# Chunk 1's attention scores as three half-precision products, with split K shared over two chunks and a second rectifier on VectorE

## The chip, the core and the metric

The kernel runs on one core of one Trainium2 chip. The metric is the device time of one execution in microseconds (us). The kernel before takes 655.71 us, the median of three runs (654.43 to 657.09). One execution was recorded by the profiler; it took 656.25 us, and its span, from the first to the last instruction, is 654.5 us.

## What is computed

Attention with a learned bias on relative positions, and behind it a layer norm and a two-layer feed-forward net (FFN), all in float32 at the interface. Four batches, eight heads, 576 positions, 64 values per head; the FFN is 512 wide with 2048 hidden values.

```
scores = q @ k.T / sqrt(64)
x      = log1p(|i - j|) / log1p(max(i, 1))            # relative position
bias   = max(x * w1 + b1, 0) @ w2                     # 32 hidden values, one bias per head
attn   = softmax(scores + bias);  a = attn @ v        # per batch and head
y      = (a - mean(a)) / sqrt(var(a) + 1e-6) * g      # over all heads of a position
out    = a + max(y @ w_ch1, 0) @ w_ch2
```

Inputs and outputs are float32, and the products must be nearly as exact. The kernel gets this from float16 in three products: a number is split into a high half-precision part and the residual, and hi*hi + hi*lo + lo*hi is summed in float32. Where it doesn't do so, it multiplies float32 operands, which TensorE executes more slowly.

## The kernel before

**Units.** The 576 query positions are cut into chunks 0 to 3 of 128 rows and chunk 4, the tail, of 64 rows. A visit is one (batch, chunk) pair, and a unit is one head of a visit (in the tail, two heads at once). There are 144 units, numbered in the order of the list `ORD`: the tails of batches 0 and 1, chunk 0, the tails of batches 3 and 2 (units 40 to 47), chunk 1 (units 48 to 79: batches 2, 3, 1, 0), chunk 2 (80 to 111) and chunk 3 (112 to 143). From one chunk to the next the batch stays the same, so its K can be kept.

**One unit.** `qk` multiplies Q and K on TensorE into PSUM; units come in pairs, two at a time. `softmax1` reads the scores and a bias tile on VectorE (line 580, scale and bias added, minimum over the row kept), takes the exponent on ScalarE (585) and a float16 copy (590); `softmax2` makes the residual on VectorE (609, 611) and sends both through a transposing DMA on the SP queue (617). `pv` multiplies by V on TensorE (627). After the eight heads of a visit VectorE scales the result (663), the layer norm follows, and the block of 128 rows enters the FFN.

**FFN.** `ffn_w1` (hps, line 855) and `ffn_w2` (y, line 884) are cut into small jobs; each step of the main loop, one per unit, issues about one of them between the attention matmuls, at a pace that spreads all jobs over the units. Between the two, ScalarE rectifies (861) and VectorE makes the residual (865). They are the larger part of TensorE's work.

**Scores.** `half(c)` tells which chunks use three half-precision products. Before, these are chunks 2 and 3 (line 513); the others multiply float32 Q and K (line 537). A chunk in half precision needs K and Q split: `split_k` for each quarter of K (ScalarE line 480, then VectorE 483) and `split_q` for each half of the heads (495, 498), both issued four steps before the first unit that uses them. Powers of two scale K and Q to the range of float16; they come from the largest magnitudes: `k_abs` and `q_abs` (VectorE line 438) on K and on blocks of Q that `q_load` brings in on the SP queue for this alone (434), and `kq_scale` at step 49, which ends in the scales `ksc`, `qsc` and the common factor `pmx`. The softmax's first step of such a unit takes its scale from `pmx` in memory.

**Bias.** 36 groups of 16 query rows: `bias_relu` makes four rectified tiles (ScalarE line 170, VectorE line 172; from step 24 on one of four is on VectorE), `bias_mm` multiplies by w2 and evicts on ScalarE to a tile that goes out to memory; later each unit's bias tile `ldb` is loaded from there and used for all four batches of a chunk. For chunks 2 and 3 the eviction multiplies by the factor of `pmx` as well (`ipf`, `cbf`), so that the bias matches the scaled scores.

**Order.** The program issues work step by step; functions for special steps hang on `at(step, ...)`. A scheduler then settles the order of each engine's instructions by its own clock. Each engine works strictly in its order; each DMA queue likewise.

Of the kernel before, what the change touches and what calls it, by code (L numbers as in the profile page):

```python
# [8 lines left out]
F32 = mybir.dt.float32  # L9
# [5 lines left out]
AF = mybir.ActivationFunctionType  # L15
# [7 lines left out]
def kernel(  # L23
# [13 lines left out]
    V, S, G, T, SY = nc.vector, nc.scalar, nc.gpsimd, nc.tensor, nc.sync  # L37
# [42 lines left out]
    GOF = [g for g, (lo, hi) in enumerate(GROUPS) for _ in range(lo, hi)]  # L80
    half4 = const.tile([128, 4], F32)
    gram = {}
    kqa = const.tile([128, 24], F32)
    kqs = const.tile([128, 8], F32)
    ksc = const.tile([128, 4], F32)
    kinv = const.tile([128, 4], F32)
# [59 lines left out]
    evi, ttri = {}, {}  # L146
# [30 lines left out]
    def bias_mm(gi):  # L177
        rs, ndve, last = rt.pop(gi)
        nrev = 16 * gi + 16
        ntot = nrev + SEQ - 16 * gi  # L180
        n = max(SEQ - 16 * gi, nrev + 1)
        if gi in gorder[12:] and n <= 512:
            ps = ps_y.tile([128, 512], F32, tag="y1", name="bps")
        else:
            ps = ps_s.tile([128, 2, 512], F32, tag="s", name="bps")
        if gi in gorder[12:]:
            flat = ps if n <= 512 else ps.rearrange("p a b -> p (a b)")
            for a in range(0, n, 512):
                b = min(n, a + 512)
                for s in range(4):  # L190
                    m = T.matmul(out=flat[32 * s:32 * s + 32, a:b], lhsT=nw2_sb, rhs=rs[s][:, a:b],  # L191
                                 start=True, stop=True)
                    after(m, last)
            ev = stage(gi, "ev")
            cb, sc = cb_sb[:, ndve:ndve + 1], ip_sb[:, gi:gi + 1]
            if half(gi // 8):
                cb, sc = cbf[:, ndve:ndve + 1], ipf[:, gi - 16:gi - 15]
            for o, i in ((ev[:, 0:nrev], flat[:, 1:nrev + 1][:, ::-1]),
                         (ev[:, nrev:ntot], flat[:, 0:ntot - nrev])):
                S.activation(o, i, AF.Identity, bias=cb, scale=sc)  # L200
        else:
            hw = ntot // 2
            for hf in range(2):
                lo, up = hf * hw, min(ntot, hf * hw + hw)
                mid = min(max(nrev, lo), up)
                for a, b in ((lo, mid), (mid, up)):
                    if a == b:
                        continue
                    for s in range(4):
                        if a < nrev:  # L210
                            src = rs[s][:, nrev - b + 1:nrev - a + 1][:, ::-1]
                        else:
                            src = rs[s][:, a - nrev:b - nrev]
                        T.matmul(out=ps[32 * s:32 * s + 32, hf, a - lo:b - lo], lhsT=nw2_sb, rhs=src,
                                 start=True, stop=True)
            ev = stage(gi, "ev")
            evi[gi] = S.activation(ev[:, 0:2 * hw].rearrange("p (a b) -> p a b", a=2), ps[:, :, 0:hw],
                                   AF.Identity, bias=cb_sb[:, ndve:ndve + 1], scale=ip_sb[:, gi:gi + 1])
        c, r0 = divmod(16 * gi, 128)
        row = NH * PITCH  # L220
        dst = nflat[c][r0 * row:(r0 + 16) * row + 16]
        dst = dst.rearrange("(k x) -> k x", k=16)[:, 0:row]
        dst = dst.rearrange("k (h j) -> k h j", h=NH)[:, :, 0:ntot]
        if c == 4:
            dst = nflat[4][r0 * PITCH:r0 * PITCH + 1]
            dst = bass.AP(dst.tensor, dst.offset, [[PITCH + 1, 16], [64 * PITCH, NH], [1, ntot]])
        (G if gi in gorder[0:12] else SY).dma_start(out=dst, in_=ev[:, 0:ntot])
# [17 lines left out]
    NAT = {(0, 4), (1, 4), (1, 0), (0, 0)}  # L245

    def half(c):
        return c in (2, 3)

    def nat_pv(b, c):  # L250
        return (b, c) in NAT
# [12 lines left out]
    def kfirst(n):  # L264
        b = ORD[n][0]
        if n == 3:
            return 0
        if n == 0 or ORD[n - 1][0] != b or half(ORD[n][1]):
            return n
        return kfirst(n - 1)  # L270

# [99 lines left out]
    def defer(fn):  # L371
        later[1].append(fn)
# [56 lines left out]
    def q_load(b, c):  # L429
        t = qhp.tile([128, 2, 4, 128], F16, tag="qh", name="qb")  # L430
        t = t.rearrange("p x a b -> p (x a b)").bitcast(F32)
        src = q_main[b, c, 0:64].rearrange("p (e h) q -> p e (h q)", e=2)
        for e in range(2):
            after(SY.dma_start(out=t[64 * e:64 * e + 64], in_=src[:, e]), ttri[max(ttri)])
        qld[b, c] = t

    def absmax(x, col):
        red = V.tensor_reduce(out=kqa[:, col:col + 1], in_=x, op=ALU.max, axis=AX.X,
                              apply_absolute_value=True)
        after(red, ttri[max(ttri)])  # L440

    def k_abs(n, g):
        absmax(kt[kuse[n], g].rearrange("p a b -> p (a b)"), 4 * ORD[n][0] + g)

    def q_abs(b, c):
        absmax(qld.pop((b, c)), 16 + 2 * b + c - 2)

    def kq_scale():
        ps = ps_y.tile([128, 512], F32, tag="y1", name="kqps")
        T.matmul(out=ps[:, 0:24], lhsT=one_sb, rhs=kqa, start=True, stop=True)  # L450
        V.tensor_reduce(out=kqs[:, 0:4], in_=ps[:, 0:16].rearrange("p (a b) -> p a b", b=4),
                        op=ALU.max, axis=AX.X)
        V.tensor_reduce(out=kqs[:, 4:8], in_=ps[:, 16:24].rearrange("p (a b) -> p a b", b=2),
                        op=ALU.max, axis=AX.X)
        V.tensor_scalar(out=kqs, in0=kqs, scalar1=2.0 ** -13, scalar2=None, op0=ALU.mult)

        def fin():
            pow2(kqs[:, 0:4], ksc, kinv)
            V.tensor_tensor(out=kqs[:, 4:8], in0=kqs[:, 4:8], in1=kinv, op=ALU.mult)
            V.tensor_reduce(out=pmx[:, 0:1], in_=kqs[:, 4:8], op=ALU.max, axis=AX.X)  # L460
            V.tensor_scalar(out=pmx[:, 0:1], in0=pmx[:, 0:1], scalar1=2.0 ** -40, scalar2=None,
                            op0=ALU.max)
            pow2(pmx[:, 0:1], pmx[:, 1:2], pmx[:, 2:3])
            V.tensor_scalar(out=qsc, in0=kinv, scalar1=pmx[:, 1:2], scalar2=None, op0=ALU.mult)
            V.tensor_scalar(out=ipf, in0=ip_sb[:, 16:32], scalar1=pmx[:, 1:2], scalar2=None,
                            op0=ALU.mult)
            V.tensor_scalar(out=cbf, in0=cb_sb, scalar1=pmx[:, 1:2], scalar2=None, op0=ALU.mult)
            V.tensor_scalar(out=pmx[:, 2:3], in0=pmx[:, 2:3], scalar1=-0.125, scalar2=None,
                            op0=ALU.mult)

        defer(fin)

    kh, qh = {}, {}

# [29 lines left out]

    def qk_half(u):
        b, c, h = units[u]
        q, kk = qh[b, c, h // 4], kh[vis[u], h // 2]
        ps = ps_s.tile([128, 2, 512], F32, tag="s", name="sps")
        first = None
        for i, (x, y) in enumerate(((0, 0), (0, 1), (1, 0))):  # L510
            for hf in range(2):
                r = slice(64 * hf, 64 * hf + 64)
                m = T.matmul(out=ps[:, hf, 0:HS], lhsT=q[r, x, h % 4], rhs=kk[r, y, h % 2],  # L513
                             start=(i == 0), stop=(i == 2), tile_position=(64 * hf, 0))
                first = first or m
        st[u] = ps
        return first
# [469 lines left out]
    def at(step, fn):  # L987
        todo.setdefault(step, []).append(fn)

    for b in range(NB):  # L990
        u0 = uv[b]
        for g in range(4):
            at(u0 - 11 + g, lambda b=b, g=g: v_max(b, g))
            at(u0 - 4 + 2 * g if b else u0 - 4 + 2 * g, lambda b=b, g=g: split_v(b, g))
    at(3, g_scale)
    for b in range(NB):
        if b < 2:
            at((3, 10)[b], lambda b=b: k_gram(ORD.index((b, 0))))
        else:
            for g in range(4):  # L1000
                at((44, 36)[b - 2] + g, lambda b=b, g=g: k_abs((7, 5)[b - 2], g))
        for c in (2, 3):
            at(36 + 2 * b + c - 4, lambda b=b, c=c: q_load(b, c))
            at(36 + 2 * b + c, lambda b=b, c=c: q_abs(b, c))
    at(49, kq_scale)
    for n, (b, c) in enumerate(ORD):
        if half(c):
            for g in range(4):
                at(ustart[b, c] + 2 * g - 4, lambda n=n, g=g: split_k(n, g))
            for hh in range(2):  # L1010
                at(ustart[b, c] + 4 * hh - 4, lambda b=b, c=c, hh=hh: split_q(b, c, hh))
# [17 lines left out]
    while u < NU + 6 or jobs or cur_job or pend or yq:  # L1029
# [62 lines left out]
        if u < 28:  # L1092
            bneed = min(bneed, 12)
        if ngroup < min(36, bneed):
            bias_relu(gorder[ngroup], 1 if u >= 24 else 2)
            ngroup += 1
        for _ in range(2):
            if wspl:
# [62 lines left out]
```

## Time and profile before

| | |
|---|---|
| runs | 654.43, 655.71, 657.09 us |
| profiled execution | 656.25 us, span 654.5 us |
| TensorE busy | 628.5 us, 96% |
| VectorE busy | 503.1 us, 77% |
| ScalarE busy | 415.1 us, 63% |
| mean granted TensorE clock | 0.995 of full speed |

Busy shares are means over the span. A matmul's end is modelled, and matmuls overlap, so the time that a group of them takes from the stream is read from the start of the group to the start of the work behind it. In the views below PE is TensorE, DVE is VectorE, ACT is ScalarE, SPq is the SP queue; a line number is that of the kernel before.

### The profile page before, as it was taken

Reading aid. Unit: us, or ns where it says so; the run is one execution under the profiler, and the core shown is the slowest. Engines: PE = TensorE matmul, PEld = TensorE weight load, DVE = VectorE, ACT = ScalarE, POOL = GpSimd, SP = SyncE. Lnnn points to the kernel's source line nnn. Section 1 sums busy time; section 2 is a strip of 40 time slices with the busy share of each in tenths; the row PEclk is TensorE's granted clock in tenths of the full one; section 3 lists DMA queues with packets and bytes.
Section 4 is the critical chain, followed back from the end, with each engine's and each line's share of the span. In section 5 each row is a group of like instructions: output and inputs, shape, how many; then the busy total and the mean of one; then the engine's idle time right before and its main releaser. Section 6 shows DMA issues by size and latency. Waiting matters only on the chain. (4 is left out here: it accounts for less than half of the span.)

```text
span 654.5 us, 19647 instructions
## 1 busy us (share of the span) xinstructions
PE 628.5 (96%) x8099; PEld 442.6 (68%) x8099; DVE 503.1 (77%) x1146; ACT 415.1 (63%) x825; POOL 65.2 (10%) x98
## 2 busy tenths in 40 slices
PE   6799999999899899999999999999999999999997
PEld 4467776866466567676777666676767776777774
DVE  6698999898678788585858787888888888885421
ACT  5565675779785345887865777878665666572110
POOL 5331330000000000000000000001011010100000
PEclk9899999999899999999999999999999999999999
DMA  8999893464799997778899988999997976674100
GB/s 333 320 396 383 289 323 134 151 120 101 159 209 230 249 226 152 166 168 159 182 184 230 194 186 147 176 180 188 221 240 183 158 174 129 125 119 90 34 17 17
DMA packets 193609, 121.72 MB, mean 186 GB/s; under 512 B 164272, under 2 KB 164400, under 8 KB 193520
## 3 DMA queue, kind: packets, MB, share of 16 engines
q1 hardware_dynamic: 189136, 104.37, 72.0%
q0 software_dynamic: 4240, 15.93, 6.7%
q8 instruction: 63, 1.03, 0.6%
q14 instruction: 26, 0.21, 0.1%
q10 hardware_dynamic: 144, 0.18, 0.1%
HBM read 64.97 MB, written 15.63 MB: 123 GB/s over the span
## 5 line engine op out<-in xcount | busy, mean ns | idle before, releaser
L855 PE MATMUL hps<-xT,w 128*128 128x128 f16 x3240 | 194.6, 219 | 4.3 <-DVE hh L865 3.9
L855 PEld LDWEIGHTS <-w 128*128 128x128 f16 x3240 | 184.1, 98 | 8.9 <-issue 6.4
L884 PE MATMUL y<-w,hh 128*128 128x512 f16 x810 | 188.4, 380 | 0.0
L585 ACT ACTIVATE t<-t,m 128x576 f32<-128x576 f32 x144 | 110.8, 769 | 114.9 <-DVE m L580 114.7
L884 PEld LDWEIGHTS <-hh 128*128 128x128 f16 x864 | 79.8, 98 | 85.6 <-issue 1.3
L609 DVE SCALAR_TENSOR_TENSOR e<-t,e 128x512 f16<-128x512 f32 x120 | 82.4, 686 | 37.1 <-ACT e L590 36.7
L590 ACT ACTIVATE e<-t 128x576 f16<-128x576 f32 x120 | 78.8, 672 | 1.2 <-DMA pt<-e 0.2
L861 ACT ACTIVATE hh<-hps 128x512 f16<-128x512 f32 x72 | 41.8, 581 | 49.0 <-PE hps L855 43.5
L865 DVE SCALAR_TENSOR_TENSOR hh<-hps,hh 128x512 f16<-128x512 f32 x72 | 49.2, 684 | 28.7 <-ACT hh L861 28.4
L627 PEld LDWEIGHTS <-pt 128*128 128x128 f16 (+1 forms) x1456 | 48.6, 100 | 25.5 <-issue 15.8
L580 DVE CUSTOM_DVE_ANT_0 t<-sps,ldb 128x576 f32<-128x576 f32 x80 | 59.3, 749 | 8.1 <-PE sps L537 5.0
L627 PE MATMUL xps<-v,pt 128*128 128x64 f16 (+1 forms) x1456 | 57.9, 194 | 4.6 <-DMA pt<-e 4.6
L895 DVE SCALAR_TENSOR_TENSOR x<-y,ycs,x 128x512 f32<-128x512 f32 x58 | 43.2, 746 | 20.3 <-PE y L884 19.7
L716 POOL TENSOR_SCALAR rs<-mv 128x1 f32<-128x1 f32 x18 | 9.3, 516 | 477.8 <-DVE mv L715 273.3
L537 PE MATMUL sps<-kf,qf 64*128 64x288 f32 (+1 forms) x384 | 54.9, 437 | 0.0
L580 DVE CUSTOM_DVE_ANT_0 t<-sps,ldb,pmx 128x576 f32<-128x576 f32 x64 | 50.1, 810 | 3.4 <-PE sps L513 1.7
L170 ACT ACTIVATE r<-psi_sb,par_sb 128x448 f32<-128x448 f32 (+23 forms) x72 | 40.2, 615 | 3.7 <-DMA nb<-ev 3.7
L483 DVE SCALAR_TENSOR_TENSOR k<-kf,ksc,k 128x576 f16<-128x576 f32 x32 | 26.1, 815 | 20.0 <-ACT k L480 19.9
L537 PEld LDWEIGHTS sps<-kf,qf 64*128 64x128 f32 (+1 forms) x384 | 26.3, 170 | 16.9 <-issue 8.3
L513 PE MATMUL sps<-k,q 64*128 64x288 f16 x384 | 29.3, 284 | 0.0
L585 ACT ACTIVATION_READ_ACCUMULATOR t<-t,m 128x1 f32 x144 | 27.1, 188 | 0.0
L513 PEld LDWEIGHTS <-q 64*128 64x128 f16 x384 | 16.0, 94 | 15.9 <-issue 9.2
(156 smaller groups left out, 771.4 us busy)
## 6 DMA issues: line engine op xcount, KB each, us to landing
kf<-in_k_s_dram SPq DMA_DIRECT2D x49, 288.0 KB, 3.4
ldb<-nb SPq DMA_DIRECT2D x40, 288.0 KB, 4.1
w<-in_w_ch_dram SPq DMA_DIRECT2D x22, 512.0 KB, 9.0
nb<-ev SPq DMA_DIRECT2D x24, 296.0 KB, 3.6
qf<-in_q_main_dram SPq DMA_DIRECT2D x24, 256.0 KB, 3.5
vf<-in_v_p_dram POOLq DMA_DIRECT2D x16, 320.0 KB, 7.7
kf<-in_k_s_dram POOLq DMA_DIRECT2D x15, 288.0 KB, 9.7
wend<-in_w_ch_dram SPq DMA_DIRECT2D x8, 512.0 KB, 5.0
```

Source lines behind the costliest of these rows:

```text
L513: m = T.matmul(out=ps[:, hf, 0:HS], lhsT=q[r, x, h % 4], rhs=kk[r, y, h % 2], start=(i == 0), stop=(i == 2), tile_position=(64 * hf, 0))
L537: m = T.matmul(out=o, lhsT=l, rhs=kk, start=True, stop=True, tile_position=(64 * hf, 64 * e))
L580: ttri[u] = V.tensor_tensor_reduce(out=halves(t), in0=ps[:, :, 0:HS], in1=halves(bias), scale=pmx[:, 2:3] if half(c) else -0.125, scalar=3e38,
L585: S.activation(t, t, AF.Exp, bias=m, scale=-1.0, accum_out=l8[b, c][:, h:h + 1])
L590: S.activation(e16[:, 0:SEQ], t, AF.Copy, scale=E_SCALE)
L609: V.scalar_tensor_tensor(out=e16[:, 640:1152], in0=t[:, 0:512], scalar=E_SCALE, in1=e16[:, 0:512], op0=ALU.mult, op1=ALU.subtract)
L627: T.matmul(out=o, lhsT=p[:, m], rhs=v[:, j, a, :], start=(i == 0), stop=(i == len(ops) - 1))
L855: T.matmul(out=h[:, idx * n:idx * n + n], lhsT=w[:, wo + kk * 128:wo + kk * 128 + 128], rhs=xT[k][:, xo + kk, 0:n], start=(i == 0), stop=( ...
L861: S.activation(hh[:, 0], h, AF.Relu)
L865: V.scalar_tensor_tensor(out=hh[:, 1], in0=h, scalar=0.0, in1=hh[:, 0], op0=ALU.max, op1=ALU.subtract)
L884: T.matmul(out=yps[k][t], lhsT=hh[:, a, o:o + 128], rhs=w[:, wo:wo + 512], start=(f == f0 and i == 0), stop=(f == f1 - 1 and i == 2))
L895: V.scalar_tensor_tensor(out=x, in0=y, scalar=ycs[:, g:g + 1], in1=x, op0=ALU.mult, op1=ALU.add)
```

## The change

Chunk 1 joins the chunks with half-precision scores. The following comes with it:

- Q's maxima are taken for chunk 1 too (12 blocks instead of 8), and loads, reductions and `kq_scale` run about six steps sooner (`kq_scale` at step 43).
- `kfirst` keeps a batch's K over the border of two half-precision chunks, and with it the split K; it is split anew only where the batch changes, or where a full-precision visit precedes.
- Chunk 1's bias tiles are made before `pmx` is known. `scale_bias` multiplies each of the eight loaded tiles in place on ScalarE, in steps 46 to 53.
- From step 50 on two of four rectifiers of a bias group are on VectorE.
- V's maxima and splits for batches 0 and 1 come two steps sooner.

```diff
-    kqa = const.tile([128, 24], F32)
+    kqa = const.tile([128, 28], F32)
...
-            if half(gi // 8):
+            if gi // 8 in (2, 3):
                 cb, sc = cbf[:, ndve:ndve + 1], ipf[:, gi - 16:gi - 15]
...
     def half(c):
-        return c in (2, 3)
+        return c in (1, 2, 3)
...
-        if n == 0 or ORD[n - 1][0] != b or half(ORD[n][1]):
+        if n == 0 or ORD[n - 1][0] != b or half(ORD[n][1]) and not half(ORD[n - 1][1]):
             return n
         return kfirst(n - 1)
...
+    def scale_bias(h):
+        raw = bt[seg[vis[ustart[2, 1]]], 1, h]
+        after(S.activation(raw, raw, AF.Copy, scale=pmx[:, 1:2]), ttri[max(ttri)])
...
-        q, kk = qh[b, c, h // 4], kh[vis[u], h // 2]
+        q, kk = qh[b, c, h // 4], kh[kuse[vis[u]], h // 2]
...
-        u0 = uv[b]
+        u0 = uv[b] - (2 if b < 2 else 0)
...
-                at((44, 36)[b - 2] + g, lambda b=b, g=g: k_abs((7, 5)[b - 2], g))
-        for c in (2, 3):
-            at(36 + 2 * b + c - 4, lambda b=b, c=c: q_load(b, c))
-            at(36 + 2 * b + c, lambda b=b, c=c: q_abs(b, c))
-    at(49, kq_scale)
+                at((39, 36)[b - 2] + g, lambda b=b, g=g: k_abs((7, 5)[b - 2], g))
+        for c in (1, 2, 3):
+            at(30 + 3 * b + c - 4, lambda b=b, c=c: q_load(b, c))
+            at(30 + 3 * b + c, lambda b=b, c=c: q_abs(b, c))
+    at(43, kq_scale)
+    for h in range(NH):
+        at(ustart[2, 1] + h - 2, lambda h=h: scale_bias(h))
     for n, (b, c) in enumerate(ORD):
         if half(c):
-            for g in range(4):
+            for g in range(4 if kuse[n] == n else 0):
                 at(ustart[b, c] + 2 * g - 4, lambda n=n, g=g: split_k(n, g))
...
-            bias_relu(gorder[ngroup], 1 if u >= 24 else 2)
+            bias_relu(gorder[ngroup], 2 if u >= 50 else 1 if u >= 24 else 2)
```

From line 473 of the kernel before on, the lines of the changed kernel are higher by 4 (580 becomes 584), and from 1006 on by 6.

How the order changes is shown at three places. The first is VectorE about unit 31, the end of batch 2's chunk 0; before:

```order
L580 ISA t,m<-sps,ldb 128x576
L580 ISA m 128x1
L895 SCALAR_TENSOR_TENSOR x<-y_2261,ycs,x 128x512
L832 SCALAR_TENSOR_TENSOR wend<-wend,ws 128x512 x2
L172 TENSOR_SCALAR r<-psi_sb,npr_sb 128x400
L609 SCALAR_TENSOR_TENSOR e_2350<-t,e_2350 128x512
L611 SCALAR_TENSOR_TENSOR e_2350<-t,e_2350 128x64
```

And now (qb is a block of Q for the maxima, kqa the table of maxima):

```order
L584 ISA t,m<-sps,ldb 128x576
L584 ISA m 128x1
L899 SCALAR_TENSOR_TENSOR x<-y_2267,ycs,x 128x512
L438 TENSOR_REDUCE kqa<-qb 128x1
L836 SCALAR_TENSOR_TENSOR wend<-wend,ws 128x512 x2
L172 TENSOR_SCALAR r<-psi_sb,npr_sb 128x400
L613 SCALAR_TENSOR_TENSOR e_2359<-t,e_2359 128x512
L615 SCALAR_TENSOR_TENSOR e_2359<-t,e_2359 128x64
```

A reduction of a Q block has come in ahead of the residual e, which the transposing DMA waits for.

The second is the SP queue at the same place; before:

```order
L227 DMA nb_136<-ev 16x8x592
L617 DMA_TRANSPOSE pt<-e_2293 128x9x128
L617 DMA_TRANSPOSE pt<-e_2350 128x9x128
L748 DMA_TRANSPOSE xT<-x_2287 128x8x128
L227 DMA nb_136<-ev 16x8x592
```

And now:

```order
L227 DMA nb_136<-ev 16x8x592
L621 DMA_TRANSPOSE pt<-e_2299 128x9x128
L434 DMA qb<-in_q_main_dram 64x512 x2
L621 DMA_TRANSPOSE pt<-e_2359 128x9x128
L752 DMA_TRANSPOSE xT<-x_2293 128x8x128
L434 DMA qb<-in_q_main_dram 64x512 x2
L227 DMA nb_136<-ev 16x8x592
```

Loads of Q blocks now stand between the transposes of the attention weights (pt).

The third is ScalarE ahead of chunk 1, after the last tail units, in the changed kernel; of these rows the K copies, the Q copy and the bias tiles (ldb) have no counterpart in the kernel before:

```order
L865 ACTIVATE hh<-hps 128x512
L747 ACTIVATE x_3654<-u,rs 128x512
L484 ACTIVATE k_3522<-kf,ksc 128x576
L589 ACTIVATE t,l_3470<-t,m 128x576
L484 ACTIVATE k_3708<-kf,ksc 128x576
L475 ACTIVATE ldb<-ldb,pmx 128x576
L594 ACTIVATE e_3660<-t 128x576
L589 ACTIVATE t,l_3470<-t,m 128x576
L475 ACTIVATE ldb<-ldb,pmx 128x576
L499 ACTIVATE q_3524<-qf,qsc 128x512
L594 ACTIVATE e_3729<-t 128x576
L865 ACTIVATE hh<-hps 128x512
```

Two K copies, two bias tiles and the first Q copy stand between the exponents of units 46 and 47 and the work behind them; the matmuls of unit 48 need the first K copy and the Q copy.

## Rows read from the trace of the kernel before

**Rows 1.** The page's first part: busy us, share of the span, instructions.
```profile
PE 628.5 (96%) x8099; PEld 442.6 (68%) x8099; DVE 503.1 (77%) x1146; ACT 415.1 (63%) x825; POOL 65.2 (10%) x98
```

**Rows 2.** Busy time by stretch: from:to, length, engines, granted clock, DMA share, GB/s.
```profile
50.00:100.00 50.00, 50.00 (x485) 38.43 (x477) 47.87 (x118) 32.84 (x76) 14.65 (x24) 1.00 0.92 331
...
140.00:170.00 30.00, 25.27 (x315) 16.61 (x311) 27.39 (x57) 28.48 (x54) 1.26 (x2) 1.00 0.41 92
170.00:180.00 10.00, 9.72 (x96) 5.71 (x98) 5.22 (x12) 6.02 (x14) 0.00 (x0) 0.83 0.97 199
235.00:253.00 18.00, 18.00 (x289) 12.52 (x287) 14.62 (x48) 7.30 (x16) 0.00 (x0) 1.00 1.05 184
253.00:319.00 66.00, 66.00 (x854) 45.59 (x849) 47.94 (x116) 55.93 (x116) 2.20 (x4) 1.00 0.79 168
...
361.00:600.00 239.00, 236.18 (x3314) 167.23 (x3312) 195.56 (x424) 161.21 (x317) 17.81 (x16) 1.00 0.87 170
```

**Rows 3.** TensorE in order of time: start, us, operation, count.
```profile
235.50 1.24 PE L537 MATMUL sps<-kf,qf 64*128 64x288 f32 x8
236.67 0.32 PE L627 MATMUL xps<-v,pt 128*64 128x64 f16 x8
...
421.67 2.75 PE L884 MATMUL y<-w,hh 128*128 128x512 f16 x12
424.26 0.51 PE L627 MATMUL xps<-v,pt 128*128 128x64 f16 x12
424.71 0.91 PE L513 MATMUL sps<-k,q 64*128 64x288 f16 x12
425.55 0.23 PE L627 MATMUL xps<-v,pt 128*128 128x64 f16 x2
```

**Rows 4.** Groups by line: operation, count | busy, mean ns | idle before, releaser.
```profile
L585 ACT ACTIVATE t<-t,m 128x576 f32<-128x576 f32 x144 | 110.8, 769 | 114.9 <-DVE m L580 114.7
...
L580 DVE CUSTOM_DVE_ANT_0 t<-sps,ldb 128x576 f32<-128x576 f32 x80 | 59.3, 749 | 8.1 <-PE sps L537 5.0 <-DMA ldb<-nb 2.3 <-DMA nb<-ev 0.4
...
L580 DVE CUSTOM_DVE_ANT_0 t<-sps,ldb,pmx 128x576 f32<-128x576 f32 x64 | 50.1, 810 | 3.4 <-PE sps L513 1.7 <-DMA nb<-ev 1.3 <-issue 0.4
...
L483 DVE SCALAR_TENSOR_TENSOR k<-kf,ksc,k 128x576 f16<-128x576 f32 x32 | 26.1, 815 | 20.0 <-ACT k L480 19.9
L480 ACT ACTIVATE k<-kf,ksc 128x576 f16<-128x576 f32 x32 | 24.3, 760 | 0.0
...
L498 DVE SCALAR_TENSOR_TENSOR q<-qf,qsc,q 128x512 f16<-128x512 f32 x16 | 11.8, 737 | 0.0
...
L495 ACT ACTIVATE q<-qf,qsc 128x512 f16<-128x512 f32 x16 | 11.3, 707 | 0.0
```

**Rows 5.** ScalarE's and VectorE's rectifiers of one bias group in order of time.
```profile
253.66 1.45 ACT L170 ACTIVATE r<-psi_sb,par_sb 128x320 f32<-128x320 f32 x3
...
253.44 0.38 DVE L172 TENSOR_SCALAR r<-psi_sb,npr_sb 128x320 f32<-128x320 f32 x1
```

**Rows 6.** The SP queue in order of time; the us of a group hold its waits.
```profile
214.45 2.82 SPq L363 DMA_DIRECT2D ldb<-nb  x5
...
217.85 2.70 SPq L434 DMA_DIRECT2D qb<-in_q_main_dram  x4
```

**Rows 7.** VectorE in order of time; in brackets the idle time before, and its releaser.
```profile
165.74 0.42 DVE L172 TENSOR_SCALAR r<-psi_sb,npr_sb 128x400 f32<-128x400 f32 x1
166.08 0.69 DVE L609 SCALAR_TENSOR_TENSOR e<-t,e 128x512 f16<-128x512 f32 x1
...
223.54 0.69 DVE L438 TENSOR_REDUCE kqa<-qb 128x1 f32<-128x512 f32 x1 [3.57 <-DMA qb<-in_q_main_dram]
```

**Rows 8.** TensorE in order of time at its waits, and the last tail pair.
```profile
170.28 0.84 PE L627 MATMUL xps<-v,pt 128*128 128x64 f16 x14 [3.24 <-DMA pt<-e]
...
225.55 0.63 PE L627 MATMUL xps<-v,wend 128*64 128x64 f16 x28 [1.36 <-DVE x L663]
226.65 1.20 PE L537 MATMUL sps<-kf,qf 64*64 64x288 f32 x16
...
229.47 1.72 PE L855 MATMUL hps<-xT,w 128*128 128x128 f16 x28 [1.05 <-DVE hh L865]
```

More of the change, by code (lines that the diff above doesn't have):

```diff
@@ L445, in q_abs @@
     def q_abs(b, c):
-        absmax(qld.pop((b, c)), 16 + 2 * b + c - 2)
+        absmax(qld.pop((b, c)), 16 + 3 * b + c - 1)
     def kq_scale():
         ps = ps_y.tile([128, 512], F32, tag="y1", name="kqps")
-        T.matmul(out=ps[:, 0:24], lhsT=one_sb, rhs=kqa, start=True, stop=True)
+        T.matmul(out=ps[:, 0:28], lhsT=one_sb, rhs=kqa, start=True, stop=True)
         V.tensor_reduce(out=kqs[:, 0:4], in_=ps[:, 0:16].rearrange("p (a b) -> p a b", b=4),
                         op=ALU.max, axis=AX.X)
-        V.tensor_reduce(out=kqs[:, 4:8], in_=ps[:, 16:24].rearrange("p (a b) -> p a b", b=2),
+        V.tensor_reduce(out=kqs[:, 4:8], in_=ps[:, 16:28].rearrange("p (a b) -> p a b", b=3),
                         op=ALU.max, axis=AX.X)
```

## The prediction

> **What bounds the kernel now.** I read the busy shares first, then busy time by stretch, then the order in time on TensorE, VectorE, ScalarE and the SP queue at the places that the change touches. In the busy shares the reader is to see TensorE at 628.5 of 654.5 us, VectorE at 503.1 and ScalarE at 415.1 [rows 1]. The shares are means, so the stretches come next [rows 2]: in 253 to 319, which is chunk 1's middle, TensorE is busy 66.00 of 66.00 us, ScalarE 55.93, VectorE 47.94; in 361 to 600 TensorE has 236.18 of 239. [...]
>
> [...]
>
> **The change part by part.**
>
> 1. Chunk 1's scores. A pair of units in full precision starts at 235.50 and the work behind it at 236.67: 1.17 us. A pair in three half-precision products takes 424.71 to 425.55: 0.84 [rows 3]. Chunk 1 has 4 batches x 8 heads = 32 units, 16 pairs: 16 x 0.33 = 5.3 us off TensorE's stream.
>
> 2. New work beside it. Split K is now made for ten (batch, chunk) visits instead of eight, 40 quarters against 32; in chunk 1 there are 16, and chunks 2 and 3 lose 8. Eight more half-Qs are split (24 against 16). One split K costs 0.760 on ScalarE and 0.815 on VectorE, one split Q 0.707 and 0.737 [rows 4]. Eight bias tiles are scaled in place on ScalarE; this operation stands nowhere in the trace, and its nearest rows are the split's copy, 0.760, and the exponent over the same 576 columns, 0.769 [rows 4]: both ends lie so close that I take 0.77. The softmax's first step with the scale from memory takes 0.810 instead of 0.749 [rows 4], 0.06 more for each of 32 units. From step 50 on one rectifier of each of 16 groups goes from ScalarE (three take 1.45, so 0.48) to VectorE (0.38) [rows 5].
> In 253 to 319 the order has 8 K splits, 4 Q splits and 2 bias tiles more, and 7 rectifiers moved. ScalarE: 55.93 + 8 x 0.760 + 4 x 0.707 + 2 x 0.77 - 7 x 0.48 = 63.0. VectorE: 47.94 + 8 x 0.815 + 4 x 0.737 + 7 x 0.38 + 16 x 0.06 = 61.0. TensorE, with eight pairs there: 66.0 - 2.6 = 63.4. So three engines are full at once. What that costs is bounded below by 50 to 100, where VectorE has 47.87 of 50, ScalarE only 32.84 and TensorE loses nothing [rows 2]: 0. Above, by 140 to 170: TensorE misses 4.73 of 30, and over 63.4 us that rate is 10.0. But there ScalarE had 28.48 of work against TensorE's 25.27, so 3.21 is plain overload, which chunk 1 doesn't have; the rest, 1.52 in 30, makes 3.2 here. The nearest row in kind is this one, without the overload, and two engines trailing can still be caught up in the lighter parts (235 to 253 has 7.30 of 18 us on ScalarE [rows 2], and six of the eight bias tiles are placed there). I take 2.0, ends 0 and 10.0.
>
> 3. The maxima. Four more Q blocks are loaded on SP and reduced on VectorE at 0.69 [rows 7], and all move about six steps ahead. Two places matter. (a) In the before, SP issues five bias loads from 214.45 on and only then, at 217.85, the last two blocks' loads [rows 6]; VectorE stands 3.57 us for them until 223.54 [rows 7], and TensorE then waits 1.36 and 1.05 us for what is queued behind on VectorE [rows 8]. In the new order the last block's load follows one bias load, and some ten VectorE rows stand between the freeing of its buffer and its reduction. TensorE can win back 0 to 2.4; I take 1.4, the wait that followed the stall directly. (b) One reduction now stands ahead of the residual at 166.08, which follows its predecessor without a gap [rows 7] and whose transpose TensorE waits 3.24 us for at 170.28 [rows 8]; a block's load also goes out on SP between the two transposes. That adds 0 to 2.0 (the reduction plus two issues, a quarter each of the 2.70 for four [rows 6]); I take 0.6, the reduction without its overlap.
>
> 4. The new wait. Scales for K and Q are needed when chunk 1 starts instead of chunk 2. VectorE computes them just after the last tail units; the Q scale comes right behind unit 47's first softmax step. Behind it on ScalarE's in-order queue stand a K copy, two bias tiles, an exponent and the Q copy, and on VectorE the two residuals; then TensorE may start unit 48. The trace of before has no such wait. Bounds: 0, since between the last tail pair, at 226.65 [rows 8], and unit 48's, at 235.50 [rows 3], TensorE has some eight us of other work, in the new order too; and 2.4, what TensorE lost behind the longest VectorE stall (1.36 + 1.05 [rows 8]). I take 0.6, nearer to nothing, because ScalarE has 7.30 of 18 us of work there [rows 2].
>
> 5. Chunks 2 and 3. ScalarE and VectorE get 8 K splits less (6.1 and 6.5 us), VectorE 9 rectifiers more (3.4). Both lie behind a TensorE that is idle 2.8 us in 239 [rows 2]: worth 0, ends -1 and +1. Four K loads less and four Q block loads more are 1152 KB against 1024 KB: 0. V's maxima and splits for two batches come two steps sooner: ScalarE work that moves out of the crowd, inside the range of step 2.
>
> Sum: -5.3 + 2.0 - 1.4 + 0.6 + 0.6 = -3.5. The profiled execution took 656.25, so 652.75; it lies 0.54 above the median of the runs shown, 655.71, and in such medians the forecast is 652.2.
>
> **The rivals.**
> A. TensorE's time is not what ends, or the crowd gives all of it back: by rows, three full engines with step 2 at 5 us and no gain from step 3. -5.3 + 5.0 + 0.6 = +0.3: 656.0. For it: 63.0 and 61.0 against 63.4 leave no slack, and both engines wait for each other in order. Against: TensorE loses 0 of 66 us with ScalarE at 85% and, in 50 to 100, with VectorE at 96%.
> B. Slower: units 56 to 67, where K splits, V maxima, V splits and bias evictions coincide. ScalarE's queue falls behind, the attention weights' transposes go out late, and TensorE stalls as at 170.28, several times. [...] It decides from the point where the crowd costs over 8 us. [...] Against B: chunk 1 has no overload by the sums, only a tie.
> C. No cost at all: step 2 is 0 and the whole stall of step 3 is gone: -5.3 - 2.4 = -7.7: 648.0.
>
> **How the numbers follow.** 0.5% of 655.71 is 3.3 us, about what a measurement of this kernel tells from no change; faster means under 652.4. The forecast (649.3 to 653.6, chance 0.50) lies at that border: 0.36 of it under, 0.14 above. A (653.6 to 659.5) has 0.26: 0.22 within, 0.04 slower. B 0.12, slower, with its time anywhere from 659.5 on. C 0.12, faster, 649.3 and under. Faster 0.36 + 0.12 = 0.48, same 0.14 + 0.22 = 0.36, slower 0.04 + 0.12 = 0.16. The range 648.0 to 658.0 reaches from C's figure through nearly all of A and leaves out B and half of C, under 0.2 together; the forecast's own is 649.3 to 653.6.
>
> **What would show it.** Right: TensorE's three-product pairs at 0.84 us 32 times in place of 16; ScalarE and VectorE each near 95% in the 63 us of chunk 1's middle with TensorE idle there about 2 us; VectorE's wait for Q blocks under 1 us; no wait over 1 us ahead of unit 48. Wrong: a TensorE wait over 3 us inside chunk 1 with a lowered clock behind it (B), idle time of some 5 us in many small waits for the FFN's residual or the transposes (A), or none at all (C).

## The result, and the profile after

The changed kernel takes 659.26 us (median of 7 runs, 657.94 to 662.02), the kernel before 655.94 in the same runs (7, 654.43 to 657.09). The ratio is 1.0056, 95% interval 1.0035 to 1.0077: 3.7 us slower, outside the predicted range of 648.0 to 658.0 and on the other side of no change. A ratio, here and below, compares all executions of the two kernels but those more than 1.5% above the fastest of their kernel; it is not the quotient of the medians.

The profiled execution of the changed kernel took 662.02 us and lies at the top of its runs: its TensorE ran at a granted clock of 0.93 in the first 48 us, that of the kernel before at 0.96, and it reaches the same place in the program 1.0 us later. Order and instructions are the same there, so this 1.0 is no cost of the change. Without it the profiled execution is 4.7 us longer than that of the kernel before, 1.0 more than the ratio says: sizes read from this profile are somewhat too large. The page's first line answers to [rows 1]:

```profile
PE 627.1 (95%) x8163; PEld 441.2 (67%) x8163; DVE 521.4 (79%) x1182; ACT 419.7 (64%) x833; POOL 65.1 (10%) x98
```

TensorE's busy time falls by 1.4 us only, since ahead of unit 46 it is 2.05 longer, 1.24 of that in the first 94 us, where the work is the same and the clock was lower. Its idle time rises from 26.0 (654.5 - 628.5) to 33.1 (660.2 - 627.1). Where it does shows when both kernels are cut at the same places of the program: the starts of the score pairs of units 46, 48, 62 and 78, and three more places that agree within 0.1 us. Chunk 1's sixteen pairs fall into seven, eight and, at the start of the fifth stretch, one. Busy time by stretch, columns as in [rows 2], of the kernel before:

```profile
180.00:226.65 46.65, 45.29 (x609) 30.55 (x605) 36.22 (x81) 29.52 (x59) 1.20 (x2) 1.00 1.08 222
226.65:235.50 8.85, 7.80 (x134) 5.41 (x133) 8.85 (x21) 4.34 (x9) 0.79 (x2) 1.00 1.15 282
235.50:291.63 56.13, 56.13 (x780) 38.86 (x779) 43.05 (x117) 39.68 (x82) 2.20 (x4) 1.00 0.81 168
291.63:354.24 62.61, 62.61 (x806) 43.25 (x802) 45.45 (x106) 46.15 (x93) 2.62 (x4) 1.00 0.92 186
354.24:406.00 51.76, 50.48 (x713) 35.92 (x713) 40.05 (x89) 38.63 (x76) 1.42 (x2) 1.00 0.96 181
406.00:600.00 194.00, 192.46 (x2696) 136.49 (x2695) 161.15 (x349) 127.16 (x252) 16.39 (x14) 1.00 0.86 169
```

The same stretches of the changed kernel:

```profile
181.20:228.74 47.54, 45.92 (x610) 31.04 (x606) 41.70 (x96) 29.48 (x60) 1.68 (x3) 1.00 1.05 234
228.74:238.29 9.55, 8.09 (x142) 5.57 (x143) 7.34 (x29) 6.25 (x12) 0.77 (x2) 1.00 1.22 216
238.29:295.77 57.48, 54.44 (x802) 37.62 (x802) 50.28 (x111) 48.77 (x99) 2.64 (x4) 1.00 0.81 174
295.77:355.62 59.85, 59.85 (x831) 41.62 (x828) 54.45 (x123) 48.41 (x96) 3.07 (x4) 1.00 0.90 183
355.62:410.40 54.78, 51.14 (x716) 35.93 (x716) 39.27 (x90) 35.45 (x69) 1.36 (x2) 1.00 0.95 177
410.40:605.50 195.10, 192.48 (x2694) 136.42 (x2693) 159.88 (x349) 121.86 (x243) 15.10 (x14) 1.00 0.82 161
```

The lengths, after less before: +0.89, +0.70, +1.35, -2.76, +3.02, +1.10. The saving is there: in the fourth stretch, units 62 to 77, eight pairs take 2.76 us less, 0.345 each, without any idle time. Ahead of it, in units 48 to 61, TensorE is idle for 3.04 us. The largest loss, 3.02, begins with chunk 1's last pair and lies behind it, where the prediction had put nothing.

The place is the border from chunk 1 to 2, units 78 to 81. TensorE in order of time, changed kernel:

```profile
361.74 2.75 PE L888 MATMUL y<-w,hh 128*128 128x512 f16 x12 [1.60 <-DVE x L899]
...
367.88 2.17 PE L859 MATMUL hps<-xT,w 128*128 128x128 f16 x36 [2.04 <-DVE hh L869]
```

VectorE there:

```profile
360.27 0.75 DVE L750 SCALAR_TENSOR_TENSOR x<-u,rs,x 128x512 f16<-128x512 f32 x1 [4.42 <-ACT x L747]
360.94 0.74 DVE L899 SCALAR_TENSOR_TENSOR x<-y,ycs,x 128x512 f32<-128x512 f32 x1
```

ScalarE, which VectorE waits for:

```profile
359.51 0.72 ACT L747 ACTIVATE x<-u,rs 128x512 f16<-128x512 f32 x1 [5.43 <-DMA pt<-e]
```

And the SP queue, whose transposes ScalarE waits for (the us of a row hold its waits):

```profile
349.29 0.52 SPq L363 DMA_DIRECT2D ldb<-nb  x1
349.86 0.42 SPq L327 DMA_DIRECT2D kf<-in_k_s_dram  x1
350.38 0.37 SPq L363 DMA_DIRECT2D ldb<-nb  x1
350.81 0.90 SPq L327 DMA_DIRECT2D kf<-in_k_s_dram  x2
351.87 1.24 SPq L621 DMA_TRANSPOSE pt<-e  x1
353.28 5.15 SPq L621 DMA_TRANSPOSE wend<-e  x1
```

Read from the top down: TensorE's y matmuls want VectorE's line 899, which reads the sum before them out of PSUM. On VectorE that stands behind the layer norm's residual (750), which waits for ScalarE's copy x (747). ScalarE stands 5.43 us before writing that copy until a transpose of attention weights has left its buffer, and the transposes stand on SP behind three K loads and two bias loads of 288 KB each, issued within 2.4 us. In the kernel before, SP issues one K load at 350.78 and the next at 358.42:

```profile
350.78 0.45 SPq L327 DMA_DIRECT2D kf<-in_k_s_dram  x1
...
352.79 4.21 SPq L617 DMA_TRANSPOSE pt<-e  x2
...
358.42 1.41 SPq L327 DMA_DIRECT2D kf<-in_k_s_dram  x1
```

So the theory to test (theory 1): the visit at the border keeps its split K and loads none, so buffers for the K of the visit behind it are free early, and its loads, which were spaced out in the kernel before, go out together and hold up the transposes. Theory 2: ScalarE and VectorE are too full in chunk 1, and the border only shows it. Theory 3, for the loss ahead of unit 48: two bias tiles stand in front of the Q copy on ScalarE.

### The profile page after: what moved, and what is told of

It is laid out like the page before. It is cut to its first block, busy times and chain, and to the rows that moved or that the text cites. A ratio compares the mean times of both kernels' runs of the same rounds, so it can differ in the third digit from the quotient of the medians.

```text
span 660.2 us, 19830 instructions
## 1 busy us (share of the span) xinstructions
PE 627.1 (95%) x8163; PEld 441.2 (67%) x8163; DVE 521.4 (79%) x1182; ACT 419.7 (64%) x833; POOL 65.1 (10%) x98
## 3 DMA queue, kind: packets, MB, share of 16 engines
q8 instruction: 64, 1.05, 0.6%
## 4 chain that ended last, share of the span: by engine, by line
PE 41%; ACT 7%; DVE 4%; issue 2%; DMA 2%; SPq 2%; POOL 1%; ACTq 0%; DVEq 0%
PE hps L859 16%; PE y L888 16%; PE xps L631 4%; PE sps L517 3%; ACT t L589 3%; DMA pt<-e 2%; PE bps L191 2%; ACT e L594 1%; DVE t L584 1%; DVE x L899 1%; POOL rs L721 1%; SPq L621 1%; ACT q L499 1%; DVE hh L869 1%; DVE e L613 1%
## 5 line engine op out<-in xcount | busy, mean ns | idle before, releaser
L584 DVE CUSTOM_DVE_ANT_0 t<-sps,ldb,pmx 128x576 f32<-128x576 f32 x96 | 75.5, 810 | 2.2 <-PE sps L517 1.5
L487 DVE SCALAR_TENSOR_TENSOR k<-kf,ksc,k 128x576 f16<-128x576 f32 x40 | 32.6, 815 | 18.6 <-ACT k L484 18.4
L517 PE MATMUL sps<-k,q 64*128 64x288 f16 x576 | 44.1, 284 | 1.8 <-ACT q L499 1.5
L584 DVE CUSTOM_DVE_ANT_0 t<-sps,ldb 128x576 f32<-128x576 f32 x48 | 35.6, 748 | 9.8 <-DMA nb<-ev 4.9
L517 PEld LDWEIGHTS <-q 64*128 64x128 f16 x576 | 23.9, 94 | 25.8 <-issue 11.4
L170 ACT ACTIVATE r<-psi_sb,par_sb 128x448 f32<-128x448 f32 (+23 forms) x56 | 32.3, 617 | 6.1 <-DMA nb<-ev 5.9
L541 PE MATMUL sps<-kf,qf 64*64 64x288 f32 (+1 forms) x256 | 35.1, 448 | 0.0
L484 ACT ACTIVATE k<-kf,ksc 128x576 f16<-128x576 f32 x40 | 30.4, 760 | 0.0
```

The source lines that it names most:

```text
L541: m = T.matmul(out=o, lhsT=l, rhs=kk, start=True, stop=True, tile_position=(64 * hf, 64 * e))
L584: ttri[u] = V.tensor_tensor_reduce(out=halves(t), in0=ps[:, :, 0:HS], in1=halves(bias), scale=pmx[:, 2:3] if half(c) else -0.125, scalar=3e38,
```

## The experiments

Each is timed against the kernel before on the same chip; the ratios are to be set beside 1.0056 (1.0035 to 1.0077), which comes from the changed kernel's own seven executions; it was not timed again beside the others. In the paced kernel and the two with K loads on POOL's queue, TensorE, ScalarE and VectorE run the same instructions in the same order as in the changed kernel. In the other kernels the scheduler also moved instructions beside the edit, so their times hold a new order too.

**K reloaded and split for each visit.**

```
-  ... or half(ORD[n][1]) and not half(ORD[n - 1][1]):
+  ... or half(ORD[n][1]):
```

> The changed kernel with one part undone: K is loaded and split again for each half-precision visit, none is kept over a border between chunks (12 split visits in place of 10). Theory 1 (the kept K lets three K loads of 288 KB go out within 2 us at each of the borders from chunk 1 to 2 and from 2 to 3; the transposes of attention weights behind them on SP come 4 to 5 us late; TensorE loses about 3.6 at the first border and 1.5 at the second): the SP row of 5.15 us for one transpose near 353 goes, and ScalarE's wait of 5.43 us near 359.5 too; the time falls by 3.5 to 5, to 654.5 to 655.7. Theory 2 (the time was lost to ScalarE and VectorE being full in chunk 1, and the border only shows it): 8 more K splits put 6.1 us on ScalarE and 6.5 on VectorE, so it is the same or slower, 659 to 662.

Measured: 659.6 against 657.38, ratio 1.0038 (1.0020 to 1.0057). The border's stall is gone: TensorE is busy 55.75 of 56 us in 354 to 410, and the one wait left there is 0.25. But by ratio only 1.2 us come back (-0.7 to 3.0 by the two intervals), not 3.5 to 5. This kernel makes 48 K splits in place of 40; that they cost the rest is not shown, since from unit 78 to 142 its profile is 3.7 us shorter than the changed kernel's (237.58 and 241.30). It shows that the kept K makes the stall, not what the stall costs.

**K kept, its next loads paced.**

```
+if key[0] in (13, 17):
+    after(ld, ttri[max(ttri)])
 kt[key[0], key[2]] = raw
```

> The changed kernel with K still kept, and the K loads of the two visits behind a kept one tied to the latest softmax step, so that on SP they stand among the transposes and not three in a row; the order on the other engines stays. Theory 1 (the burst of loads delays the transposes): the waits of 5.43 us on ScalarE near 359.5 and 3.97 near 483.4 shrink under 1.5, TensorE loses under 1 at each border; 654.3 to 655.8, 3.5 to 5 under the changed kernel. Theory 2 (full engines in chunk 1): the same as the changed kernel within 1, 658.3 to 660.3, and the waits on ScalarE stay over 3.

Measured: 657.91 against 657.38, ratio 1.0004 (0.9983 to 1.0025), 3.4 us under the changed kernel's ratio (1.5 to 5.4 by the two intervals, which do not meet), just short of the 3.5 to 5 expected. The stretch of 3.02 is gone; here are 345 to 395 of the changed kernel, with 3.64 us of idle TensorE, and then of the paced one:

```profile
345.00:395.00 50.00, 46.36 (x644) 32.37 (x642) 37.64 (x84) 30.20 (x62) 2.93 (x4) 1.00 1.00 192
```

```profile
345.00:395.00 50.00, 50.00 (x682) 34.60 (x680) 40.43 (x93) 33.17 (x67) 2.92 (x4) 1.00 1.03 206
```

SP at the border of the paced kernel:

```profile
348.34 1.54 SPq L365 DMA_DIRECT2D ldb<-nb  x2
350.04 1.49 SPq L623 DMA_TRANSPOSE pt<-e  x1
351.69 1.40 SPq L623 DMA_TRANSPOSE wend<-e  x1
```

The row of 5.15 us is 1.40, and ScalarE waits 0.76, for POOL, in place of 5.43. At the second border it waits 0.76 too, in place of 3.97, and TensorE has no wait there. From unit 78 to 82 this kernel takes 14.07 us, the changed kernel 18.03. TensorE, ScalarE and VectorE have the same work in the same order, so theory 2 falls for these 3.4 us.

**Kept K alone, in the kernel before.** The same edit of the K visits, chunk 1's scores in full precision.

> The kernel before with one part of the change alone: split K kept over the border from chunk 2 to 3 (chunk 1's scores stay in full precision, one K visit of four loads less). Theory 1 (the kept K makes a burst of loads at the border): the burst on SP appears near that border, and the time is 1 to 2 above the kernel before, 657 to 658. Theory 2 (chunk 1's crowd): 0 to 0.5 under the kernel before, 655.4 to 656, since four splits less are made.

Measured: 656.8 against 657.38, ratio 0.9999 (0.9977 to 1.002). Theory 1's number missed, though the burst is there. SP:

```profile
467.83 0.42 SPq L327 DMA_DIRECT2D kf<-in_k_s_dram  x1
468.35 0.37 SPq L363 DMA_DIRECT2D ldb<-nb  x1
468.78 0.90 SPq L327 DMA_DIRECT2D kf<-in_k_s_dram  x2
469.84 5.25 SPq L617 DMA_TRANSPOSE pt<-e  x2
```

Its first load goes out 7.0 us before ScalarE wants the layer norm's buffer, in the changed kernel 4.9 us before at this border and 4.2 at the first: ScalarE waits 1.91 us for the transposes, TensorE 0.80. What a burst costs depends here on how soon behind it a transpose is wanted: ScalarE waits 5.43, 3.97 and 1.91 us for 4.2, 4.9 and 7.0. The second border alone is worth too little to be measured (1.5 us either way).

**Queue or transfers?** The same three loads on POOL's queue, first left free:

```
-ld = ring(u).dma_start(...)
+ld = (G if key[0] in (13, 17) else ring(u)).dma_start(...)
```

> The changed kernel with the K loads of the two visits behind a kept one issued on POOL's queue in place of SP's; they go out as early as before, three in a row, only not ahead of transposes on the same queue. Theory 1a (the transposes wait in SP's own queue behind the loads): the SP row of 5.15 us and the waits of 5.43 and 3.97 us on ScalarE go, and the time is 0 to 1 us above the kernel before, as for the paced kernel (ratio 1.000 to 1.0015). Theory 1b (the three K transfers fill the DMA engines and the transposes' own transfers are slow, whichever queue issues the loads): one transpose's issue still takes 4 to 5 us near 353, and the time stays 3 to 4 us above the kernel before (ratio 1.0045 to 1.006).

Measured: 657.43 against 657.05, ratio 1.0013 (0.9992 to 1.0033), and ScalarE's wait is 2.48. This looks like theory 1a, but the run doesn't separate the two, since on POOL the loads went out apart, not in a row as expected:

```profile
327.33 0.63 POOL L327 DMA_DIRECT2D kf<-in_k_s_dram  x1 [7.11 <-DMA qf<-in_q_main_dram]
333.76 0.54 POOL L327 DMA_DIRECT2D kf<-in_k_s_dram  x1 [5.80 <-DVE k L487]
339.79 0.54 POOL L327 DMA_DIRECT2D kf<-in_k_s_dram  x1 [5.49 <-DVE k L487]
```

The two later rows wait for the K split (line 487) that frees a buffer. So the buffers come free some 6 us apart, long before 350, and it is the order on SP that puts the loads together in the changed kernel. On POOL they were then held back to the moment of the burst:

```
+key[0] in (13, 17) and after(ld, ttri[min(max(ttri), 76 if key[0] < 15 else 108)])
```

> The changed kernel with the K loads of the two visits behind a kept one on POOL's queue, and held back to the softmax step of unit 76 (of unit 108 at the second border), so that three go out in a row at the moment at which SP issues them in the changed kernel, but from another queue. On POOL alone they had gone out 6 us apart from 327 on, so that run did not tell the two apart. Theory 1a (the transposes wait behind the loads in SP's own order): no transpose takes over 3 us near 353, and the time is 0 to 1 us above the kernel before. Theory 1b (while three K transfers of 288 KB lie in the DMA engines, a transpose's issue is held up, whichever queue they came from): one transpose's issue takes 4 to 5 us again, ScalarE's wait is over 4, and the time is 2.5 to 4 us above the kernel before.

Measured: 660.81 against 656.97, ratio 1.0054 (1.0026 to 1.0083): as slow as the changed kernel. Its executions spread widely, from 658.07 to 669.74; the profiled one took 664.77, so the stall below is a large one. POOL's burst, then SP's transposes, then ScalarE and TensorE:

```profile
351.45 1.69 POOL L327 DMA_DIRECT2D kf<-in_k_s_dram  x3 [30.35 <-DVE m L584]
```

```profile
357.04 10.22 SPq L621 DMA_TRANSPOSE pt<-e  x2
```

```profile
364.64 0.68 ACT L594 ACTIVATE e<-t 128x576 f16<-128x576 f32 x1 [4.36 <-DMA wend<-e]
```

```profile
370.51 4.00 PE L859 MATMUL hps<-xT,w 128*128 128x128 f16 x36 [5.33 <-DVE hh L869]
```

The transposes stand on a queue that holds none of the three loads and are held up all the same, 10.22 us for two against 3.33 in the paced kernel: theory 1b. POOL did nothing else while it held them back, so it delayed no other work. The three loads from POOL are slower than SP's (median to landing 9.8 us, 5.3 in the changed kernel's burst), so the size of this stall is its own. At the second border the same burst from POOL held up the transposes less, and TensorE shows no wait:

```profile
484.49 6.19 SPq L621 DMA_TRANSPOSE pt<-e  x2
```

**Ahead of unit 48.** The bias tiles one step later (`h - 1` for `h - 2`):

> The changed kernel with the bias tiles scaled one step later, so that the first two do not stand ahead of unit 48's Q copy on ScalarE. Theory 3 (the wait of 1.47 us ahead of unit 48, behind the Q copy, is made by the two bias tiles of 0.77 each): 1.0 to 1.5 under the changed kernel, 657.8 to 658.3, with that wait under 0.5. Rival (the wait is for the scales themselves, which VectorE gives late): the same within 0.4, 658.9 to 659.7, and the wait stays over 1.

Measured: 659.55 against 657.38, ratio 1.0040 (1.0017 to 1.0063), some 1 us under the changed kernel, within both intervals: inconclusive in time. One step later takes only one of the two tiles from ahead of the Q copy; the other still stands there. In the profile the wait is 0.89 in place of 1.47, so one tile of 0.76 accounts for 0.58 of it:

```profile
238.50 0.54 PE L517 MATMUL sps<-k,q 64*128 64x288 f16 x6 [0.89 <-ACT q L499]
```

Without the tiles, on the paced kernel:

> The paced kernel without the scaling of the eight bias tiles; the bias of chunk 1's last scores is left unscaled, so this part of the computation is left out. It takes 8 x 0.77 us off ScalarE between 234 and 250. Theory 3 (the bias tiles ahead of the Q copy make the wait of 1.47 before unit 48 and some of the waits for hh and xT between 240 and 262): TensorE gains 1.5 to 2.5, 1 to 2 us under the kernel before. Rival (the scales come late from VectorE, and ScalarE has room there): the wait of 1.47 stays over 0.8, a gain under 0.8, 0 to 0.5 above the kernel before.

Measured: 656.31 against 657.05, ratio 0.9994 (0.9974 to 1.0014): 0.7 under the paced kernel by ratio (1.2 above to 2.6 under by the intervals), which holds both the rival's gain and theory 3's. The wait is 0.41 in place of 1.47, as theory 3 said:

```profile
242.59 1.33 PE L519 MATMUL sps<-k,q 64*128 64x288 f16 x12 [0.41 <-ACT q L501]
```

With two, one and no tile ahead of the Q copy, in an order that is otherwise the same at that place, the wait is 1.47, 0.89 and 0.41. So the tiles make most of the wait; what it is worth in time these runs don't tell.

**The Q blocks on POOL's queue**, on the paced kernel (`G.dma_start` for `SY.dma_start` in `q_load`):

> The paced kernel with the Q blocks for the maxima loaded on POOL's queue in place of SP's, so that the last block's load no longer stands behind K and bias loads. Theory (VectorE's wait of 1.8 to 3.5 us for the last block, near 218, is SP's queue, and TensorE's 1.1 + 1.1 us near 220 to 223 come from it): the wait falls under 1, TensorE gains 1 to 2: 1 to 2 us under the kernel before. Rival (the wait is for the buffer, which two reductions free late, or for the transfer): the wait stays over 1.5, and the time is within 0.7 of the paced kernel, 0 to 1 above the kernel before.

Measured: 656.71 against 657.05, ratio 1.0000 (0.9975 to 1.0025). VectorE's wait for the last block is gone, as are TensorE's waits at 220 and 223. In the profile this kernel reaches unit 48's pair at 237.12, the paced one at 239.00; in the timings nothing of it can be told.

**The rectifiers undone**, on the paced kernel:

```
-bias_relu(gorder[ngroup], 2 if u >= 50 else 1 if u >= 24 else 2)
+bias_relu(gorder[ngroup], 1 if u >= 24 else 2)
```

> The paced kernel with the rectifiers undone: from step 50 on one of each group on VectorE and three on ScalarE, as before. By the sums of the prediction ScalarE gets 7 x 0.48 = 3.4 us more in 253 to 319, 66.4 against TensorE's 63.4. Theory (ScalarE is then over its limit): TensorE idles 2 to 4 us more in chunk 1, 2 to 4 us above the paced kernel. Rival (the crowd is made of waits at single places, not of sums): within 1 us of the paced kernel.

Measured: 659.53 against 657.05, ratio 1.0040 (1.0021 to 1.0060), 2.4 us over the paced kernel's. The size is the theory's, the place is not: in 253 to 319 TensorE is busy 64.08 of 66 us with them undone and 63.83 in the paced kernel, ScalarE 62.48 and 60.52. The loss stands in chunk 2:

```profile
420.07 2.84 PE L861 MATMUL hps<-xT,w 128*128 128x128 f16 x48 [1.23 <-DVE hh L871]
460.17 1.33 PE L861 MATMUL hps<-xT,w 128*128 128x128 f16 x21 [1.06 <-DVE hh L871]
```

The paced kernel waits 0.22 at the first of these and nothing at the second.

**All three remedies**: paced loads, Q blocks and bias tiles on POOL (`G.tensor_scalar` for the tiles).

> The kernel with paced K loads and Q blocks loaded on POOL's queue, and the eight bias tiles scaled by POOL in place of ScalarE. POOL is busy 2.6 of 65 us in 235 to 300, so its work should be covered. If ScalarE's eight tiles of 0.77 in front of the Q copy and among the splits cost what the run without them showed against the paced kernel (about 0.6 us) and the Q blocks on POOL's queue are worth 0 to 0.5, the time is 0.5 to 1.5 us under the kernel before (ratio 0.9977 to 0.9992). Rival (POOL takes several us for a tile of 128 x 576, and the softmax of units 50 to 55 waits for it, or VectorE slows down beside it): 1 to 4 us above the kernel before.

Measured: 656.02 against 656.97, ratio 0.9990 (0.9967 to 1.0013), inside the expected figures and not to be told from the kernel before. A pair of tiles takes POOL 3.46 to 4.19 us against 0.76 for one on ScalarE, all of it covered.

## Why the prediction was wrong, by its steps

Read from the profile between equal places of the program, with 0.345 us for each of the sixteen pairs, the terms of the prediction's sum came out as follows:

| step | taken | in the profile |
|---|---|---|
| 1, chunk 1's scores (16 pairs) | -5.3 | -5.5 |
| 2, new work in chunk 1 | +2.0 | +2.9 |
| 3a, the stall for the last Q block | -1.4 | 0.0 |
| 3b, the reduction ahead of the residual | +0.6 | +0.3 |
| 4, the wait at unit 48 | +0.6 | +2.35 |
| 5, chunks 2 and 3 | 0 | +4.7 |
| sum | -3.5 | +4.7 |

**Step 5 failed, and decides the sign.** It put chunks 2 and 3 at 0 (-1 to +1) and "Four K loads less and four Q block loads more" at 0, by counting bytes. It did not ask when loads go out whose buffers come free earlier. Behind chunk 1 the stretches got 3.02 + 1.10 = 4.1 us longer (4.7 to the end of the program, when the saving of chunk 1's last pair is not set against it); the paced kernel takes 3.4 us of the total back by ratio, with the same bytes, and is then level with the kernel before. In its profile the same two stretches are 50.91 and 193.50, 1.35 shorter than before: without the burst, step 5 would have erred on the other side. On SP's queue the new order had these K loads together; the prediction looked there at Q and bias loads alone.

**Step 1 was right.** 0.33 a pair was taken, 0.345 measured over eight. Rival A's first reason, that TensorE's time is not what ends, falls: units 62 to 77 got shorter by all of it, 2.76 us.

**Step 2 was nearly right in size.** These rows answer to [rows 2]:

```profile
140.00:170.00 30.00, 26.52 (x320) 17.21 (x318) 27.85 (x56) 27.88 (x52) 1.26 (x2) 1.00 0.55 108
170.00:180.00 10.00, 8.47 (x86) 5.84 (x90) 5.39 (x14) 6.80 (x15) 0.00 (x0) 0.83 0.97 212
...
253.00:319.00 66.00, 63.84 (x887) 43.66 (x884) 60.08 (x138) 60.54 (x123) 2.64 (x4) 1.00 0.82 169
```

TensorE idles 2.16 us in 253 to 319 where 2.0 was taken; ScalarE has 60.54 for 63.0, VectorE 60.08 for 61.0. A bias tile takes 0.760 (0.77 taken). The costs that "nearest rows" gave held. Over all of units 48 to 77 the crowd cost somewhat more: the fifteen pairs should have saved 5.2 and saved 1.41, and of the 3.8 between them 0.9 is in the waits of step 4.

**Step 3a failed.** It gave -1.4 for a stall won back. The wait for the last Q block shrank from 3.57 to 1.78 and didn't go. TensorE's 1.36 and 1.05 [rows 8] went, but it got 0.99 and 0.63, the first behind an earlier block that VectorE waited 1.15 for:

```profile
218.23 0.69 DVE L438 TENSOR_REDUCE kqa<-qb 128x1 f32<-128x512 f32 x1 [1.78 <-DMA qb<-in_q_main_dram]
```

```profile
206.99 2.17 PE L859 MATMUL hps<-xT,w 128*128 128x128 f16 x36 [0.99 <-DVE hh L869]
...
222.72 2.84 PE L859 MATMUL hps<-xT,w 128*128 128x128 f16 x48 [0.63 <-DVE hh L869]
```

The stretch got longer by 0.89, and with the next one, up to unit 48, by 1.59; 1.47 of that is step 4's wait, so nothing was won here. In the paced kernel, with the same order here, the wait was 3.45. Two K loads still stood ahead of that block on SP; "some ten VectorE rows" between buffer and use were not time enough. By the diff the Q reductions also do not all move about six steps: the last goes from step 45 to 42 and `kq_scale` from 49 to 43, so the scales, which came four steps behind the last block, now come one step behind it.

**Step 3b** took 0.6; TensorE idles 3.48 + 1.53 = 5.0 us in 140 to 180, and 4.73 + 0.28 = 5.0 before [rows 2]: 0. Between equal places of the program this part is 0.3 longer. In place of the 3.24 us wait stand two, 1.70 and 1.28.

**Step 4 was mis-sized, just inside its ends.** 0.6 was taken, "nearer to nothing", up to 2.4. The waits at unit 48 and right behind are 1.47, 0.37, 0.24 and 0.27, 2.35 together:

```profile
238.29 0.42 PE L517 MATMUL sps<-k,q 64*128 64x288 f16 x4 [1.47 <-ACT q L499]
239.08 0.67 PE L517 MATMUL sps<-k,q 64*128 64x288 f16 x8 [0.37 <-DVE q L502]
240.41 2.17 PE L859 MATMUL hps<-xT,w 128*128 128x128 f16 x36 [0.24 <-DVE hh L869]
...
243.53 0.63 PE L631 MATMUL xps<-v,pt 128*64 128x64 f16 x28 [0.27 <-DVE x L694]
```

A light engine (7.30 of 18 us busy) said nothing of an in-order queue in which two bias tiles stand ahead of the one copy that TensorE needs.

Of the rivals A gave the time a place (653.6 to 659.5 holds 659.26, by its slowest part), but not for its reason: chunk 1 still saved 1.41, and what was lost most was lost behind it. B had the sign and a nearby kind of stall (late transposes), but the wrong place and cause: the stall is not in units 56 to 67 and not ScalarE's queue, and the granted clock is 1.00 over 345 to 395, so the lowered clock that was to show it is missing too. Rest: most of step 1's saving is spent by +1.6 ahead of unit 48 and 3.0 of idle time in units 48 to 61, so that even without the burst the change gains nothing that can be measured. Which of those waits could be bought out stays open: each remedy alone is within the measurement's uncertainty.

## What to carry to other kernels

When a change makes buffers come free earlier, ask what is loaded into them, when it now goes out, and which short transfer on the path stands behind: here the same bytes cost 3.4 us more in a burst than paced. A wait on an in-order engine is priced from the instructions that stand ahead of the one needed, not from that engine's busy share: here it was 1.47, 0.89 and 0.41 us with two, one and no bias tile ahead. Another issuing queue did as well as the pace only while the loads went out spaced (ratio 1.0013, in a burst 1.0054).

## What the runs showed of the hardware that was not expected

Three K loads of 288 KB issued within 1.7 us from POOL stretched two transposes on SP to 10.22 us, where the paced kernel's two take 3.33; one of the transposes beside the burst landed 12.7 us after its issue, in the paced kernel 3.5. The same burst 130 us later gave 6.19 and cost TensorE no wait, so one such stall is no fixed price. Left to go out 6 us apart from the same queue, the same loads cost nothing that can be measured (ratio 1.0013, 0.9992 to 1.0033). In the run with POOL's burst the granted clock was 0.51 in 370.5 to 374.5, behind TensorE's wait of 5.33 us, while behind the changed kernel's waits of 1.60 and 2.04 us it stayed at 1.00.

```profile
370.50:374.50 4.00, 3.99 (x39) 3.98 (x39) 3.52 (x8) 2.61 (x6) 0.00 (x0) 0.51 1.21 284
```
